# FNet block with modulated MLP on one core: the columns of 1+ca and sa turned by a 32x32 transpose, other buffers for the chunks of ga and sb, other assumed landing times

## The chip, the cores and the metric

The kernel runs on one core of a Trainium2 chip. A core has a matrix engine (TensorE, PE in the profile), a vector engine (VectorE, DVE), an activation engine (ScalarE, ACT), a general engine (GpSimd, POOL) and a synchronisation engine (SyncE, SP) that here only issues transfers (DMAs). Each engine takes its instructions in the order in which they were written. The metric is the device time of one execution in microseconds.

## The reference

```python
x = A_x                                              # 2048 x 1024
sa, ca, ga, sb, cb, gb = (silu(c) @ w_mod).reshape(6, 1024)
h = layernorm(x) * (1 + ca) + sa
x = x + ga * real(DFT_seq(DFT_hidden(h)))            # Cr@(h Dr) - Ci@(h Di)
h = layernorm(x) * (1 + cb) + sb
x = x + gb * (gelu(h @ w1 + b1) @ w2 + b2)           # 1024 -> 3584 -> 1024
```

Six rows of 1024 numbers, each a product of the vector silu(c) with 1024 columns of `w_mod`, scale and shift what the two large blocks work on. The DFT matrices (2048x2048 and 1024x1024, real and imaginary) are inputs.

## The kernel before, in words

**Stages on PE.** All matmuls are 128x128 by 128x512 in fp16, with operands split into a hi and a lo half. Stage 1 multiplies the normalised x by the DFT over the sequence, in four blocks of 512 output positions. Block 0 is done plainly (L1268): ops 0 to 15, 48 matmuls each. Blocks 1 to 3 are done in a scheme with seven products in place of eight (L1320): ops 16 to 99, 28 a block, 24 matmuls each. Then come the DFT over the hidden dimension (L1552) and the two matrix products of the MLP (L1735, L1844).

**What an op needs.** For every op a piece of the DFT matrix is loaded (`craw`, L801; `rawc`, L815), in blocks 1 to 3 combined on DVE (`comb_c`, L827; the sums are named T1 to T4), and split: ACT makes the hi half (L787), DVE the lo half (L790). PE starts an op when its lo half is there. Blocks 1 to 3 also read sums and differences of x: `s_tasks` makes them (DVE L753 to L756, ACT's hi half L764, DVE's lo half L767) and POOL stores them to DRAM (tiles `s_81` to `s_84`, L771), from where SP loads them again (L854). `u_tasks` does the like with the results of block 0 and later ones (ACT L897, DVE L900 and L912, POOL store L902).

**The modulation rows.** `pair_tasks(j, ...)` makes two rows of 1024 at a time: ca and sa (j = 0), ga and sb (1), A0 and A1 (2: the sa row carried through the hidden DFT), cb and gb (3). For each row SP loads eight raw chunks of 128x1024 (`load`, L499 from `w_mod`, L496 from the DFT), DVE multiplies each by a column of silu(c) and adds it up (`mul`: L503 the first, L505 the rest), and POOL adds the 128 partitions together in a tree of seven accumulating DMAs (L519: 64 rows on 64, 32 on 32, down to 1), then puts the rows to DRAM (`put`, L526). For j = 0, `get` (L539, L540) loads the two rows back as columns, one number of 4 bytes at a time, and one broadcast number (`m1`); `largest` (L545, L546), a reduction over partitions on POOL (L560) and `scales` (L549 to L556, with a helper at L203) scale them. Pair 2 needs the scaled columns.

The raw chunks go to places in one large SBUF tile, `arena`, by the table `RING`. A load waits until the previous user of its place is through (`used`, `free`, `was`). Chunks 6 and on of pair 1 (ga 6, ga 7, and of sb also the third and fourth of each four) use the places 184 and 188, where the rows of ca and sa stood; so they wait for the puts of ca and sa.

**What sets the order.** A planner on the host builds lists of `Task`s, each with an engine, a cost, what it depends on and a due time relative to PE (`t_op`). It picks tasks against a modelled clock and writes them out, engine by engine; what it assumes for the time from issue to landing of a transfer stands in `LANDS`. The order is fixed once the kernel is built; on the chip every instruction waits, with all behind it on its engine, until what it depends on is there.

Of the kernel before, what the change touches and what calls it, by code (L numbers as in the profile page):

```python
# [9 lines left out]
F32 = mybir.dt.float32  # L10
# [3 lines left out]
ALU = mybir.AluOpType  # L14
RED = bass_isa.ReduceOp
AX = mybir.AxisListType

P = 128
S = 2048
D = 1024  # L20
F = 3584
NS = S // P
ND = D // P
# [13 lines left out]
def kernel(ctx, tc, x, cre, cim, dre, dim, w1, b1, w2, b2, c, wm, out):  # L37
# [137 lines left out]
    def quad(g):  # L175
# [13 lines left out]
        [dram.tile([P, 4, 2, 512], F16, tag=f"dc_{m}_{ri}", name=f"dc_{m}_{ri}") for ri in range(2)] for m in range(7)  # L189
    ]  # L190
    arow_d = [dram.tile([1, D], F32, tag=f"arow_{n}", name=f"arow_{n}") for n in range(2)]
    row_d = {
        n: dram.tile([1, D], F32, tag=f"row_{n}", name=f"row_{n}") for n in ("ca", "sa", "ga", "sb", "cb", "gbb", "gb")
    }
    w1_d = [dram.tile([P, 7, 2, 512], F16, tag=f"w1_{g}", name=f"w1_{g}") for g in range(14)]
    w2_d = [dram.tile([P, 7, 2, 2, 512], F16, tag=f"w2_{v}", name=f"w2_{v}") for v in range(7)]
# [259 lines left out]


    scol, cc = mk([P, ND], F32, "scol"), mk([P, ND], F32, "cc")
    cols = mk([P, 2 * ND], F32, "cols")
    cs, csa = cols[:, 0:ND], cols[:, ND : 2 * ND]  # L460
    m1 = mk([P, 6], F32, "m1")
    ones = at(O_SO[0], 512)
# [1 line left out]
    def idle_pe(n):  # L464
# [8 lines left out]
    ROWS = (184, AUX[2], AUX[0], 64)  # L473
    RING = (
        [(192, 196, 172, 176, 180)[q % 5] if q < 10 else (192, 196)[q % 2] for q in range(16)],
        [(192, 196)[q % 2] if q < 6 else (192, 196, 184, 188)[q % 4] for q in range(16)],
        [(AUX[2], AUX[3], 64, 68)[q % 4] for q in range(16)],
        [AUX[q % 4] for q in range(16)],
    )
# [1 line left out]
    def pair_tasks(j, due, free):  # L481
# [6 lines left out]
        for q in range(2 * ND):  # L488
            i, k = divmod(q, ND)
            o = RING[j][q]  # L490
            name, b = names[i], at(o, 1024)
            col = csa if name in src else scol

            def load(name=name, k=k, b=b):
                if name in src:
                    sp.dma_start(b, dri[src[name]][:, k, :])  # L496
                else:
                    m = MODS.index(name)
                    sp.dma_start(b, wm[:, k, m * D : (m + 1) * D])  # L499

            def mul(i=i, k=k, b=b, col=col):
                if k == 0:
                    dve.tensor_scalar(rows[i], b, col[:, 0:1], None, op0=ALU.mult)  # L503
                else:
                    dve.scalar_tensor_tensor(rows[i], b, col[:, k : k + 1], rows[i], op0=ALU.mult, op1=ALU.add)  # L505

            loads.append(Task("dma", 1.5, load, [used.get(o) or free[o]], ("wm", name, k)))
            LANDS[loads[-1].key] = 4.0 if j else 6.0
            deps = [loads[-1].key, ("row", "sa", "end") if name in src else None]
            if k == 0:  # L510
                deps.append(free.get(place + 4 * i))
            muls.append(Task("dve", 1.3 if k else 0.75, mul, deps, ("row", name, k)))
            used[o] = muls[-1].key
# [4 lines left out]
        while n:  # L518
            f = lambda n=n: gp.dma_start(both[0:n], both[n : 2 * n], accum_op=ALU.add)  # L519
            t.append(Task("pool", 0.7, f, [last, muls[ND - 1].key], ("tree", j, n)))  # L520
            last = t[-1].key
            LANDS[last] = 3.0
            n //= 2

        def put(v, dst, dep, end=None):
# [2 lines left out]
            return u  # L528

        r = [v[0:1, :] for v in rows]  # L530
        row = [row_d[n][:, :] for n in names] if j != 2 else [a[:, :] for a in arow_d]
        if j == 0:
            t += [put(r[0], row[0], last, ("put", "ca")), put(r[1], row[1], last, ("put", "sa"))]
            dep = [t[-2].key, t[-1].key]

            def get():
                for name, o in (("ca", cs), ("sa", csa)):
                    v = row_d[name][0].rearrange("(k p) -> p k", p=P)
                    sp.dma_start(o, v, allow_slow_non_contiguous=True)  # L539
                sp.dma_start(m1[:, 4:5], row_d["ca"][0][0:1].partition_broadcast(P))  # L540

            m, pm, sd, iu = (m1[:, n : n + 1] for n in range(4))

            def largest():
                dve.tensor_scalar(cs, cs, 1.0, None, op0=ALU.add)  # L545
                dve.tensor_reduce(m, cols, axis=AX.X, op=ALU.max, apply_absolute_value=True)  # L546

            def scales():
                dve.tensor_scalar(m, m, 1e-30, None, op0=ALU.max)  # L549
                pow2(pm, m)  # L550
                dve.reciprocal(sd, pm)
                dve.tensor_scalar(sd, sd, SD, None, op0=ALU.mult)
                dve.tensor_scalar(iu, pm, 2.0**5 / SD, None, op0=ALU.mult)
                dve.tensor_scalar(cols, cols, sd, None, op0=ALU.mult)
                dve.tensor_scalar(m1[:, 4:5], m1[:, 4:5], 1.0, -1.0, op0=ALU.add, op1=ALU.mult)
                dve.tensor_scalar(m1[:, 4:5], m1[:, 4:5], sd, None, op0=ALU.mult)  # L556

            u = chain(
                ("dma", 1.5, get), ("dve", 0.4, largest),
                ("pool", 0.7, lambda: gp.partition_all_reduce(m, m, P, RED.absmax)), ("dve", 1.3, scales),  # L560
            )
            u[0].deps = tuple(dep)
            LANDS[u[0].key] = 6.0
            LANDS[u[2].key] = 1.0
            u[-1].key = ("row", "sa", "end")
            t += u
        elif j == 1:
            k_ = Task(
                "dve", 0.9, lambda: dve.tensor_scalar(r[0], r[0], m1[0:1, 3:4], None, op0=ALU.mult),
                [last, ("row", "sa", "end")],  # L570
            )
            t += [put(r[1], row[1], last), k_, put(r[0], row[0], k_.key, ("row", "sb", "end"))]
        elif j == 3:
            b = at(60, 1024)[0:1, :]
            l = Task("dma", 1.5, lambda: sp.dma_start(b, b2), [muls[-1].key])
            LANDS[l.key] = 5.0
            p = put(r[1], row[1], last)
            k_ = Task("dve", 0.9, lambda: dve.tensor_scalar(r[0], r[0], 1.0, None, op0=ALU.add), [last])
            m = Task("dve", 1.3, lambda: dve.tensor_tensor(b, b, r[1], op=ALU.mult), [l.key, last])
            t += [l, p, k_, put(r[0], row[0], k_.key), m, put(b, row_d["gbb"][:, :], m.key, ("row", "gb", "end"))]  # L580
        else:
            t += [put(v, o, last, ("row", n, "end")) for v, o, n in zip(r, row, names)]
# [346 lines left out]
    def d_tasks(n):  # L929
# [11 lines left out]
        for h in (1, 0):  # L941
            f = lambda h=h: sp.dma_start(b[h], dri[ri][:, c_ + 4 * h, :])
            ls.append(Task("dma", 1.5, f, [dep, ("row", "A0", "end") if n == 1 else ("g1", 15)]))
            LANDS[ls[-1].key] = 4.0
        if n % 4 == 0:
            dep = ("row", "A1", ND - 1) if n == 0 else ("dd", n - 1)
            z = Task("dma", 1.5, lambda: sp.dma_start(d0, dri[ri][0, 0].partition_broadcast(P)), [dep])
# [644 lines left out]
    load_halves([c0_raw(0)[:, 0:512], xf(8)], [cre[0, :, 0, :], x[8]])  # L1592
    sp.dma_start(c0_raw(0)[:, 512:1024], cre[0, :, 8, :])
    dve.memset(warm, 1.0)
    act.dma_start(cc[:, :], c)
    act.activation(warm[:, :], warm[:, :], AF.Silu)
    act.activation(scol[:, :], cc[:, :], AF.Silu)
# [38 lines left out]
                push("comb", "comb", cb_[kp][j], t_op(opn(tb, m, kp)) - (30.0, 25.0)[j])  # L1636
    pair_tasks(0, t_op(5), {o: ("op", 2) for o in RING[0]})
    was = {o: ("row", "sa", k) for o, k in ((192, 6), (196, 7))}
    was.update({184: ("put", "ca"), 188: ("put", "sa")})
    pair_tasks(1, t_op(9), {**was, AUX[2]: ("op", 6), AUX[3]: ("op", 7)})  # L1640
    s_end = {64: ("st", "s", 14), 68: ("st", "s", 15), AUX[0]: ("op", 14), AUX[1]: ("op", 15)}
    s_end.update({AUX[2]: ("row", "sb", "end"), AUX[3]: ("row", "sb", "end")})
# [379 lines left out]
    for kind, k in seq:  # L2022
# [47 lines left out]
        else:  # L2070
            v = k
# [59 lines left out]
```

## Time and profile before

| | us |
|---|---|
| median of 3 runs (lowest, highest) | 1990.1 (1988.07, 1990.2) |
| profiled execution, whole | 1989.65 |
| its span in the trace | 1987.7 |
| PE busy | 1939.7 (98%) |
| DVE busy | 1437.1 (72%) |
| ACT busy | 842.2 (42%) |
| POOL busy | 190.9 (10%) |
| stage 1, plain block: ops 2 to 15 | 33.29 to 196.90 |
| stage 1, blocks 1 to 3: ops 16 to 99 | 196.90 to 651.76 |

The granted clock of PE was 0.993 of full over the span. The page gives for each engine its busy time, for each wait the instruction that waited and the one that released it, and for DMAs the time from issue to landing. A timeline row has start, duration, engine, line, operation and, in brackets, the idle time ahead of it with its releaser. `SPq` is SP's queue of DMA issues: a long duration of three issues there means that one of them waited. Names like `arena<-in_wm_dram` read "written from".

### The profile page before, as it was taken

What the parts mean: (1) busy time and instruction counts of PE and PEld (TensorE: products, weight loads), DVE (VectorE), ACT (ScalarE), POOL (GpSimd) and SP (SyncE); (2) the same over time, 40 slices, a digit from 0 to 9 for tenths busy, and PEclk for the clock granted to TensorE, in tenths of its full rate; (3) what the DMA queues carried; (4) which work ended last, traced back from release to release, by engine and by line L of the source; (5) the groups of instructions that cost most, each with busy time, mean ns of one, the idle gap of its engine ahead of it and who ended that gap; (6) DMA issues with size and microseconds to landing.
All of it is one profiled execution on the core that took longest, in us unless ns stands there. A gap on an engine that the chain in (4) does not pass through costs nothing. (4 is left out here: it accounts for less than half of the span.)

```text
span 1987.7 us, 23757 instructions
## 1 busy us (share of the span) xinstructions
PE 1939.7 (98%) x8979; PEld 882.1 (44%) x8979; DVE 1437.1 (72%) x1872; ACT 842.2 (42%) x1081; POOL 190.9 (10%) x316
## 2 busy tenths in 40 slices
PE   9979989999999999999999999999999999999999
PEld 3434434444444444444444444444444444444444
DVE  8866787998885467877678998989873353553566
ACT  7522433544522345554577566456233312312311
POOL 0031212211101112211120000000000000000000
PEclk9999999999999999999999999999999999999999
DMA  8478798688787877868665555444477332432323
GB/s 331 156 241 265 244 334 282 242 288 291 257 310 259 322 244 269 297 222 300 261 229 178 179 196 175 138 170 151 168 229 213 118 97 83 127 101 69 112 75 85
DMA packets 146200, 412.92 MB, mean 208 GB/s; under 512 B 19115, under 2 KB 19179, under 8 KB 141998
## 3 DMA queue, kind: packets, MB, share of 16 engines
q1 hardware_dynamic: 117782, 316.23, 46.9%
q0 software_dynamic: 28160, 95.18, 14.3%
q8 instruction: 70, 1.15, 0.2%
q14 instruction: 44, 0.36, 0.1%
q10 hardware_dynamic: 144, 0.00, 0.0%
HBM read 271.88 MB, written 135.30 MB: 205 GB/s over the span
## 5 line engine op out<-in xcount | busy, mean ns | idle before, releaser
L1735 PE MATMUL ps<-arena 128*128 128x512 f16 x2352 | 511.9, 380 | 2.2 <-ACT arena L1757 2.2
L1844 PE MATMUL ps<-arena 128*128 128x512 f16 x2352 | 511.1, 379 | 2.7 <-DVE arena L1890 1.2
L1320 PE MATMUL ps<-arena 128*128 128x512 f16 x2016 | 439.5, 381 | 15.5 <-DVE arena L790 10.5
L1735 PEld LDWEIGHTS <-arena 128*128 128x128 f16 x2352 | 230.5, 98 | 280.7 <-issue 4.8
L1844 PEld LDWEIGHTS <-arena 128*128 128x128 f16 x2352 | 230.0, 98 | 281.3 <-issue 3.7
L1890 DVE SCALAR_TENSOR_TENSOR arena<-ps,i4c,arena 128x1024 f32<-128x1024 f32 x179 | 229.3, 1281 | 146.4 <-PE ps L1844 141.2
L1320 PEld LDWEIGHTS <-arena 128*128 128x128 f16 x2016 | 197.7, 98 | 257.2 <-issue 15.9
L1552 PE MATMUL ps<-arena 128*128 128x512 f16 x1344 | 294.0, 381 | 2.7 <-ACT arena L1568 2.7
L390 ACT ACTIVATE arena<-arena,shc 128x512 f16<-128x512 f32 (+1 forms) x115 | 116.0, 1018 | 282.2 <-PE ps L1844 189.2
L1552 PEld LDWEIGHTS <-arena 128*128 128x128 f16 x1344 | 131.9, 98 | 160.0 <-issue 5.3
L1268 PE MATMUL ps<-arena 128*128 128x512 f16 x768 | 169.2, 382 | 19.4 <-DVE arena L790 18.0
L415 DVE TENSOR_TENSOR arena<-arena 128x512 f32<-128x512 f32 (+1 forms) x228 | 171.1, 753 | 4.3
L402 DVE SCALAR_TENSOR_TENSOR arena<-arena,shc 128x512 f16<-128x512 f32 (+1 forms) x115 | 128.5, 1121 | 39.1 <-ACT arena L390 38.9
L787 ACT ACTIVATE arena<-arena 128x1024 f16<-128x1024 f32 x99 | 102.1, 1049 | 112.0 <-PE ps L1320 68.9
L1761 DVE TENSOR_TENSOR arena<-arena,ps 128x512 f32<-128x512 f32 x84 | 57.5, 684 | 110.9 <-PE ps L1735 107.1
L1754 ACT ACTIVATE arena<-arena,b1s,i1c 128x512 f32<-128x512 f32 x84 | 68.3, 813 | 138.3 <-DVE arena L1761 138.3
L1268 PEld LDWEIGHTS <-arena 128*128 128x128 f16 x768 | 75.1, 98 | 113.5 <-issue 21.9
L790 DVE SCALAR_TENSOR_TENSOR arena<-arena 128x1024 f16<-128x1024 f32 x99 | 118.8, 1217 | 8.0 <-ACT arena L787 7.8
L897 ACT ACTIVATE arena<-arena 128x1024 f16<-128x1024 f32 x56 | 58.6, 1052 | 113.5 <-DMA u<-arena 63.9
L900 DVE TENSOR_TENSOR arena<-arena 128x1024 f16<-128x1024 f32 x56 | 67.6, 1218 | 19.8 <-ACT arena L897 19.8
L390 ACT ACTIVATE arena<-arena,s1c 128x512 f16<-128x512 f32 (+1 forms) x70 | 60.9, 885 | 44.1 <-DVE arena L415 25.5
L402 DVE SCALAR_TENSOR_TENSOR arena<-arena,s1c 128x512 f16<-128x512 f32 (+1 forms) x70 | 66.4, 959 | 10.1 <-ACT arena L390 10.1
(165 smaller groups left out, 1384.9 us busy)
## 6 DMA issues: line engine op xcount, KB each, us to landing
w<-arena SPq DMA_DIRECT2D x64, 512.0 KB, 5.0
arena<-w SPq DMA_DIRECT2D x119, 256.0 KB, 2.7
u<-arena POOLq DMA_DIRECT2D x56, 512.0 KB, 5.9
arena<-u SPq DMA_DIRECT2D x112, 256.0 KB, 4.0
arena<-w SPq DMA_DIRECT2D x56, 512.0 KB, 3.4
arena<-in_wm_dram SPq DMA_DIRECT2D x48, 512.0 KB, 5.6
arena<-s SPq DMA_DIRECT2D x48, 512.0 KB, 6.1
arena<-in_cim_dram SPq DMA_DIRECT2D x32, 512.0 KB, 7.1
```

Source lines behind the costliest of these rows:

```text
L390: act.activation(o[m][0], q(j), AF.Copy, **sc)
L402: dve.scalar_tensor_tensor(o[m][1], q(j), scale, o[m][0], op0=ALU.mult, op1=ALU.subtract)
L415: dve.tensor_tensor(q(d), q(a), q(b), op=op)
L787: h = Task("act", 1.15, lambda: act.activation(o[:, :, 0], s2, AF.Copy, scale=SC), list(deps) + free)
L790: dve.scalar_tensor_tensor(o[:, :, 1], s2, SC, o[:, :, 0], op0=ALU.mult, op1=ALU.subtract)
L1268: pe.matmul(bank_of(d_), hleft(d_, s, kp, a), cop(n)[:, s, b], start=(kp == 0 and s == 0 and a == 0 and b == 0), stop=(kp == 7 and s == 1 ...
L1320: pe.matmul(bank_of(st + ch), left, cop(n)[:, s, b], start=(start and kp == 0 and s == 0 and a == 0 and b == 0), stop=(kp == 3 and s == 1 ...
L1552: pe.matmul(bank_of(bk), up(N)[:, c_, a], dp(n)[:, c_, w], start=(start and ri == 0 and c_ == 0 and i == 0), stop=(ri == 1 and c_ == 3 and ...
L1735: pe.matmul(ps.rearrange("p (k t) -> p k t", k=4), w1c[:, m, s, a, d * P : (d + 1) * P], zc(m)[:, b, :, d, :], start=(start and d == 0 and ...
L1754: act.activation(dst, src, AF.Gelu_apprx_tanh, scale=inv, bias=b1s[:, 2 * p + j : 2 * p + j + 1])
L1844: pe.matmul(t[:, j], hidc[:, c_, m, a, k * P : (k + 1) * P], w2c[:, m, c_, w], start=(start and c_ == 0 and n == 0), stop=(c_ == 1 and n = ...
L1890: lambda: dve.scalar_tensor_tensor(dst, ps[b], inv, dst, op0=ALU.mult, op1=ALU.add), kp[b],
```

## The change

It has three parts.

1. The rows ca and sa go to one DRAM tile `ca_d` of 2x1024. `get` loads them as eight DMAs of 8 rows by 128 bytes into a tile `turned` of 128x32, beside the broadcast as before. `largest` first transposes `turned` to `cols` on DVE, in blocks of 32x32, and the reduction and the scaling take the first 16 columns of it. `turned` is cleared once at the start.
2. The raw chunks of ga and sb go to the places 192, 196 and 216 in turn. 216 has no earlier user, and none of the loads waits for the puts of ca and sa.
3. `LANDS`, by which the planner orders, has for the chunks of the rows 7.0 us (before 4.0, for pair 0 6.0), for the levels of the tree 8.5 down to 2.5 (before 3.0 each), and 6.0 for the loads of the hidden DFT (before 4.0).

```diff
+    ca_d = dram.tile([2, D], F32, tag="ca_sa", name="ca_sa")
...
-    cols = mk([P, 2 * ND], F32, "cols")
+    turned, cols = mk([P, 32], F32, "turned"), mk([P, 32], F32, "cols")
...
-        [(192, 196)[q % 2] if q < 6 else (192, 196, 184, 188)[q % 4] for q in range(16)],
+        [(192, 196, 216)[q % 3] for q in range(16)],
...
-            LANDS[loads[-1].key] = 4.0 if j else 6.0
+            LANDS[loads[-1].key] = 7.0
...
-            LANDS[last] = 3.0
+            LANDS[last] = {64: 8.5, 32: 6.5, 16: 5.5, 8: 5.0, 4: 4.5, 2: 4.0, 1: 2.5}[n]
...
             def get():
-                for name, o in (("ca", cs), ("sa", csa)):
-                    v = row_d[name][0].rearrange("(k p) -> p k", p=P)
-                    sp.dma_start(o, v, allow_slow_non_contiguous=True)
-                sp.dma_start(m1[:, 4:5], row_d["ca"][0][0:1].partition_broadcast(P))
+                v = ca_d.rearrange("r (k q j) -> q r k j", q=4, j=32)
+                for q in range(4):
+                    for r_ in range(2):
+                        sp.dma_start(turned[32 * q + 8 * r_ : 32 * q + 8 * r_ + 8, :], v[q, r_])
+                sp.dma_start(m1[:, 4:5], ca_d[0][0:1].partition_broadcast(P))
...
             def largest():
+                dve.transpose(cols, turned)
                 dve.tensor_scalar(cs, cs, 1.0, None, op0=ALU.add)
-                dve.tensor_reduce(m, cols, axis=AX.X, op=ALU.max, apply_absolute_value=True)
+                dve.tensor_reduce(m, cols[:, 0 : 2 * ND], axis=AX.X, op=ALU.max, apply_absolute_value=True)
...
-            LANDS[ls[-1].key] = 4.0
+            LANDS[ls[-1].key] = 6.0
...
+    dve.memset(turned, 0.0)
...
-    was.update({184: ("put", "ca"), 188: ("put", "sa")})
+    was[216] = None
```

By the third part the planner's order changes on DVE, ACT, POOL and SP, from about op 4 of stage 1 to the end of stage 1; PE's does not. In the new kernel lines stand one to six further down: L505 is L506, L790 is L795, L767 is L772, L900 is L905, L912 is L917, L499 is L500, L815 is L820, L519 is L520, L771 is L776.

On DVE, around ops 12 and 13 (lo halves L790), ahead of the change. `scol` marks a multiplication of a raw chunk:

```order
L505 SCALAR_TENSOR_TENSOR arena_65<-arena_65,scol_190 128x1024
L790 SCALAR_TENSOR_TENSOR arena_65<-arena_65 128x2x512
L912 TENSOR_TENSOR arena_65<-arena_65 128x8x128
L755 TENSOR_TENSOR arena_65<-arena_65 128x512
L900 TENSOR_TENSOR arena_65<-arena_65 128x4x2x128
L545 TENSOR_SCALAR cols_192<-cols_192 128x8
L546 TENSOR_REDUCE m_6_193<-cols_192 128x1
L505 SCALAR_TENSOR_TENSOR arena_65<-arena_65,scol_190 128x1024
L503 TENSOR_SCALAR arena_65<-arena_65,scol_190 128x1024
```

And now, from op 12's half (the first L795) through op 13's (the second) to the columns:

```order
L795 SCALAR_TENSOR_TENSOR arena_65<-arena_65 128x2x512
L917 TENSOR_TENSOR arena_65<-arena_65 128x8x128
L506 SCALAR_TENSOR_TENSOR arena_65<-arena_65,scol_189 128x1024 x3
L905 TENSOR_TENSOR arena_65<-arena_65 128x4x2x128
L758 TENSOR_TENSOR arena_65<-arena_65 128x512
L917 TENSOR_TENSOR arena_65<-arena_65 128x8x128
L759 TENSOR_TENSOR arena_65<-arena_65 128x512
L795 SCALAR_TENSOR_TENSOR arena_65<-arena_65 128x2x512
L905 TENSOR_TENSOR arena_65<-arena_65 128x4x2x128
L506 SCALAR_TENSOR_TENSOR arena_65<-arena_65,scol_189 128x1024 x3
L549 STREAM_TRANSPOSE cols_192<-turned_191 128x32
L550 TENSOR_SCALAR cols_192<-cols_192 128x8
```

Before, `largest` stood between ops 12 and 13; now it stands, with the transpose, between ops 13 and 14, and six multiplications of raw chunks stand between op 12 and it.

On SP, from a pair of loads for time block 1 (`in_cre_dram 128x1024`; `in_wm_dram` marks the raw chunks) past the columns, before:

```order
L815 DMA arena_65<-in_cre_dram 128x1024 x2
L499 DMA arena_65<-in_wm_dram 128x1024 x3
L815 DMA arena_65<-in_cre_dram 128x1024 x2
L539 DMA cols_192<-row_ca 128x8x1
L539 DMA cols_192<-row_sa 128x8x1
L540 DMA m_6_193<-row_ca 128x1
L499 DMA arena_65<-in_wm_dram 128x1024 x2
L801 DMA arena_65<-in_cim_dram 128x2x512
L499 DMA arena_65<-in_wm_dram 128x1024 x5
```

and now:

```order
L500 DMA arena_65<-in_wm_dram 128x1024 x6
L820 DMA arena_65<-in_cre_dram 128x1024 x2
L806 DMA arena_65<-in_cim_dram 128x2x512
L500 DMA arena_65<-in_wm_dram 128x1024 x3
L543 DMA turned_191<-ca_sa 8x32 x8
L544 DMA m_7_193<-ca_sa 128x1
L806 DMA arena_65<-in_cim_dram 128x2x512
L500 DMA arena_65<-in_wm_dram 128x1024
```

Before, nine raw chunks of ga and sb were still to be loaded behind the columns; now one is.

On POOL, in tree 1 (the rows ga and sb), before:

```order
L519 DMA arena_65<-arena_65 64x2048
L519 DMA arena_65<-arena_65 32x2048
L519 DMA arena_65<-arena_65 16x2048
L771 DMA s_81<-arena_65 128x1024
L771 DMA s_82<-arena_65 128x1024
L771 DMA s_84<-arena_65 128x1024
L771 DMA s_83<-arena_65 128x1024
L519 DMA arena_65<-arena_65 8x2048
```

and now:

```order
L520 DMA arena_65<-arena_65 64x2048
L520 DMA arena_65<-arena_65 32x2048
L776 DMA s_81<-arena_65 128x1024
L776 DMA s_82<-arena_65 128x1024
L776 DMA s_84<-arena_65 128x1024
L776 DMA s_83<-arena_65 128x1024
L520 DMA arena_65<-arena_65 16x2048
L776 DMA s_81<-arena_65 128x1024
```

The four s stores went ahead of the tree's third level.

More of the change, by code (lines that the diff above doesn't have):

```diff
@@ L191 @@
     arow_d = [dram.tile([1, D], F32, tag=f"arow_{n}", name=f"arow_{n}") for n in range(2)]
+    ca_d = dram.tile([2, D], F32, tag="ca_sa", name="ca_sa")
     row_d = {
-        n: dram.tile([1, D], F32, tag=f"row_{n}", name=f"row_{n}") for n in ("ca", "sa", "ga", "sb", "cb", "gbb", "gb")
+        n: dram.tile([1, D], F32, tag=f"row_{n}", name=f"row_{n}") for n in ("ga", "sb", "cb", "gbb", "gb")
     }
@@ L530, in pair_tasks @@
         r = [v[0:1, :] for v in rows]
-        row = [row_d[n][:, :] for n in names] if j != 2 else [a[:, :] for a in arow_d]
+        row = [ca_d[i : i + 1, :] for i in range(2)] if j == 0 else (
+            [row_d[n][:, :] for n in names] if j != 2 else [a[:, :] for a in arow_d]
+        )
         if j == 0:
@@ L553, in scales @@
                 dve.tensor_scalar(iu, pm, 2.0**5 / SD, None, op0=ALU.mult)
-                dve.tensor_scalar(cols, cols, sd, None, op0=ALU.mult)
+                dve.tensor_scalar(cols[:, 0 : 2 * ND], cols[:, 0 : 2 * ND], sd, None, op0=ALU.mult)
                 dve.tensor_scalar(m1[:, 4:5], m1[:, 4:5], 1.0, -1.0, op0=ALU.add, op1=ALU.mult)
```

## The prediction

> **What bounds the kernel now.** I read the page's head first, then PE's waits, then PE's timeline, and only then the queues of the engines that PE waited for.
>
> ```profile
> span 1987.7 us, 23757 instructions
> PE 1939.7 (98%) x8979; PEld 882.1 (44%) x8979; DVE 1437.1 (72%) x1872; ACT 842.2 (42%) x1081; POOL 190.9 (10%) x316
> ```
>
> PE works for 98% of the span, so a change that removes no matmul can win only what PE idles, and what it runs slower after idling. The waits say where:
>
> ```profile
> PE ps L1268 <- DVE arena L790: 18.0, 4, 12.5
> PE ps L1320 <- DVE arena L790: 10.5, 5, 5.7
> PE ps L1320 <- DMA arena<-s: 4.9, 3, 2.1
> ```
>
> Columns: total us, times, longest. Nearly all of it is stage 1 waiting for an op's lo half (L790). The timeline puts the places:
>
> ```profile
> 33.29 104.08 PE L1268 MATMUL ps<-arena 128*128 128x512 f16 x480 [0.40 <-DVE arena L790]
> 149.91 12.37 PE L1268 MATMUL ps<-arena 128*128 128x512 f16 x48 [12.55 <-DVE arena L790]
> 165.92 31.13 PE L1268 MATMUL ps<-arena 128*128 128x512 f16 x143 [3.64 <-DVE arena L790]
> 196.90 36.93 PE L1320 MATMUL ps<-arena 128*128 128x512 f16 x169
> ...
> 257.30 18.45 PE L1320 MATMUL ps<-arena 128*128 128x512 f16 x72 [5.75 <-DVE arena L790]
> 282.27 10.30 PE L1320 MATMUL ps<-arena 128*128 128x512 f16 x47 [1.01 <-DVE arena L790]
> ...
> 389.74 262.18 PE L1320 MATMUL ps<-arena 128*128 128x512 f16 x1214
> 651.76 10.52 PE L1552 MATMUL ps<-arena 128*128 128x512 f16 x48
> ```
>
> Unhindered, ops 2 to 11 take 104.08/10 = 10.41 us for 48 matmuls, and the later run 262.18/1214 = 0.2160 us a matmul. Against that pace:
> - Loss A: from op 11's end (33.29 + 104.08 = 137.37) to 196.90 are 59.53 us for four ops, 41.6 at pace: 17.9 lost, 16.2 of it in the two waits and the rest in the slower 48 matmuls behind the longer one (12.37).
> - Loss B: from 196.90 to 651.76 are 454.86 us for 2016 matmuls, 435.4 at pace: 19.5 lost. Up to 282.27 (14 ops of 24, 72.6 at pace) it is 12.8; the other 6.7 come after.
>
> Together 37.4: more the change cannot win, since PE's own order and all work after 651.76 stay.
>
> Why op 12 is late stands in SP's queue, POOL's and DVE's:
>
> ```profile
> 117.94 24.13 SPq L499 DMA_DIRECT2D arena<-in_wm_dram  x3
> 143.13 0.51 SPq L539 DMA_DIRECT2D cols<-row_ca  x1
> 143.73 3.79 SPq L539 DMA_DIRECT2D cols<-row_sa  x1
> 147.56 4.81 SPq L540 DMA_DIRECT2D m<-row_ca  x1
> ```
>
> ```profile
> 140.01 0.52 POOL L526 DMA_DIRECT2D row_ca<-arena  x1 [1.98 <-DMA arena<-arena]
> ```
>
> ```profile
> 106.06 1.22 DVE L790 SCALAR_TENSOR_TENSOR arena<-arena 128x1024 f16<-128x1024 f32 x1
> 147.44 1.29 DVE L505 SCALAR_TENSOR_TENSOR arena<-arena,scol 128x1024 f32<-128x1024 f32 x1 [8.41 <-DMA arena<-in_wm_dram]
> 148.64 1.22 DVE L790 SCALAR_TENSOR_TENSOR arena<-arena 128x1024 f16<-128x1024 f32 x1
> 153.82 0.17 DVE L546 TENSOR_REDUCE m<-cols 128x1 f32<-128x16 f32 x1 [0.21 <-DMA cols<-row_sa]
> 157.82 1.28 DVE L505 SCALAR_TENSOR_TENSOR arena<-arena,scol 128x1024 f32<-128x1024 f32 x1 [3.83 <-DMA arena<-in_wm_dram]
> ```
>
> SP's third raw load here (chunk 6 of ga) sits until 142.1 (117.94 + 24.13) for the put of ca, whose row's place it takes. DVE's multiplication of that chunk starts at 147.44, and op 12's lo half stands right behind it. Then the element-wise column loads hold SP to 152.4; the next chunk is late by 3.83 more and op 13 (after a 3.64 wait at 165.92) with it.
>
> **The change, part by part.** *Other places.* Ga and sb chunks no longer wait for the puts of pair 0, so the waits of 8.41 and 3.83, and the 1.27 that follows, have no cause. What DVE then has to do before op 12 I take from the new order: nine instructions of 128x1024 (L767, L900, L912), four of 128x512, five L505 and one L503.
>
> ```profile
> L900 DVE TENSOR_TENSOR arena<-arena 128x1024 f16<-128x1024 f32 x56 | 67.6, 1218 | 19.8 <-ACT arena L897 19.8
> L755 DVE TENSOR_TENSOR arena<-arena 128x512 f32<-128x512 f32 x8 | 5.5, 690 | 0.2
> L505 DVE SCALAR_TENSOR_TENSOR arena<-arena,scol 128x1024 f32<-128x1024 f32 x42 | 53.9, 1282 | 24.0 <-DMA arena<-in_wm_dram 23.1
> L503 DVE TENSOR_SCALAR arena<-arena,scol 128x1024 f32<-128x1024 f32 x6 | 4.5, 748 | 1.3 <-DMA arena<-in_wm_dram 1.3
> ```
>
> 9 x 1.22 + 4 x 0.69 + 5 x 1.28 + 0.75 = 20.9 us, with op 12's own half 22.1. Op 11's half ended at 107.28; one L505 and one L767 more now stand ahead of it (2.5), so op 12 is ready at 107.28 + 2.5 + 22.1 = 131.9 if nothing waits; PE wants it at 137.37. The same count from op 12 to op 15 gives 10.1, 11.0 and 8.9 us, 30.0 in all against 31.2 on PE. So DVE has 5.5 us to spare, and waits are what remains:
>
> ```profile
> DVE arena L505 <- DMA arena<-in_wm_dram: 14.3, 3, 8.4
> DVE arena L767 <- ACT arena L764: 7.8, 2, 4.2
> ```
>
> From 109 to 166 us these and L503's 1.3 make 23.4; without the 13.5 named, 9.9 stay, and they lie ahead of op 12. If all stay, op 12 is 4.4 late and the slower clock behind a pause costs 12.37 - 10.41 = 2.0 on top, and some 2 at op 14: residual of A 0 to 8. I take 3, since the L767 waits are for s stores that POOL now issues earlier.
>
> *The transfers* must fit too.
>
> ```profile
> 95.00:180.00 85.00, 68.81 (x310) 30.53 (x308) 57.23 (x64) 23.64 (x25) 20.12 (x33) 0.92 0.79 261
> 180.00:233.00 53.00, 52.87 (x246) 23.86 (x244) 32.52 (x35) 22.37 (x27) 15.99 (x26) 1.00 0.66 186
> 233.00:303.00 70.00, 56.75 (x246) 24.47 (x245) 62.47 (x55) 20.77 (x21) 6.24 (x10) 0.95 0.97 344
> ```
>
> The last two columns are DMA share and GB/s. 85 x 0.79 = 67 us of full DMA work, now in 85 - 15 = 70 us: 0.96, no more than the 0.97 seen in the lowest row. It fits, barely, which is a second reason for 3 and not 0.
>
> *Columns.* Two element-wise loads become eight of 8x128 bytes and a transpose.
>
> ```profile
> cols<-row_ca SPq DMA_DIRECT2D x1, 4.0 KB, 10.2
> row_ca<-arena POOLq DMA_DIRECT2D x1, 4.0 KB, 1.6
> ```
>
> No such load is in the trace. Its landing lies between the contiguous 4 KB (1.6) and the element-wise one (10.2); I take 3, nearest the contiguous kind. SP's issue is 0.3 to 0.55 each (the 0.51 above), nine in 3 to 5 us instead of 9.2 (143.13 to 152.37). Tree 0 I leave ending as before, since between its levels there still stand groups of s and u stores: put at 140 to 142, columns at 148 to 150. `largest` and `scales` with what lies between need 5.5 us ahead of op 14's half, and PE wants op 14 at 137.37 + 2 x 10.41 = 158.2: they must be there by 151.5. Two us to spare; cost 0, up to 7 with the longer landing. The transpose (128x32) lies between the reduction's 0.17 and the 0.69 of 128x512; I take 0.2, hidden in DVE's spare time, and 0.7 at most without it. The new memset runs beside the first loads, 0.1 if uncovered.
>
> The Trainium skill speaks against this part ("DMA: Bandwidth & Descriptors", section "Rules for kernel authors"): many small transfers are to be made one, since little ones pay mostly overhead. The same table says that a strided last dimension lowers to one descriptor per element, which is for the change; the 10.2 above agrees. The page's section "Anatomy of one DMA" gives about 2 us fixed for each DMA from GpSimd; for nine in series an estimate from it is 18 us.
>
> *Assumed landings.* They alter the order of DVE, ACT, POOL and SP up to some 640 us. What of it reaches PE I see in POOL's queue before stage T3 of time block 1:
>
> ```profile
> 188.76 0.80 POOL L519 DMA_DIRECT2D arena<-arena  x1 [7.59 <-DMA arena<-arena]
> 194.25 0.78 POOL L519 DMA_DIRECT2D arena<-arena  x1 [4.69 <-DMA arena<-arena]
> 195.24 2.24 POOL L771 DMA_DIRECT2D s<-arena  x4 [0.21 <-issue]
> ```
>
> ```profile
> 200.66 1.23 DVE L767 TENSOR_TENSOR arena<-arena 128x1024 f16<-128x1024 f32 x1 [8.77 <-ACT arena L764]
> ```
>
> Four s stores stand behind tree 1's third level; ACT cannot reuse their buffer, and DVE waits 8.77 for ACT. In the new order they stand behind the second level: not at 195.24 but between the start of that level's issue (188.76) and its end (189.56), so 5.7 to 6.5 sooner; I take 6, and as much of the wait goes. So DVE reaches its unbroken stretch (62.47 of 70 us busy from 233 to 303) about 6 us earlier against PE. Its work up to op 29 counts the same in both orders to half a us. The 12.8 then shrink to 6.8. The later 6.7 hang on loads of s and of the hidden-DFT matrix that wait for PE or come when DMA is full; I leave them. Residual of B: 13.5. Its ends: 19.5 (nothing won) and 4 (little but the 4.9 of waits for s).
>
> *Sum*, from the profiled execution (1989.65 us, its span and 1.95 around it, 0.45 below the median 1990.1): 17.9 - 3 + 19.5 - 13.5 = 20.9, so 1968.75; with the 0.45, 1969.
>
> **Rivals.**
> 1. *A is won, B is not.* PE comes to time block 1 some 15 us sooner, while transfers there already run at 0.97 and DVE at 62.47 of 70. Then 1990.1 - 15 = 1975, or 1980 if A keeps 8 and B gives 0. For it: nothing is removed from DVE's or DMA's work there. Against: DMA had only 0.66 from 180 to 233. The Trainium skill's same page, section "Bandwidth", has HBM per core bind at about 358 GB/s; by that the 24.1 MB of the 70 us (70 x 344 GB/s) take at least 67 us, an estimate that would leave 3 of the 12.8 to win in place of 6. The 344 agrees with such a limit.
> 2. *B is nearly emptied.* DVE's lead lasts through time block 1: residuals 2 and 4, 1990.1 - 31.4 = 1958. Against: the rows 257.30 and 282.27 show PE waiting for a DVE that the windows show busy nine tenths.
> 3. *Eight small loads in series.* If each of nine pays an issue of 0.5 and a landing of 1.6 one behind the other, 2.1 each, columns are there at 143 + 19 = 162 and op 14's half at 167.5, 9 late; with 2 for the clock behind the pause 20.9 - 11 = 9.9 are left, 1980. Against: the three loads of before did not wait for each other's landing (issues 143.13 and 143.73, landings of 10). It decides once columns land after 151.5. The coalescing rule cited above is this rival.
> The next rival rests on two rows of SP:
>
> ```profile
> SPq L496 <- DMA row_ga<-arena: 8.3, 1, 8.3
> ```
>
> ```profile
> 227.18 0.80 SPq L496 DMA_DIRECT2D arena<-in_dre_dram  x2
> ```
>
> 4. *Slower: tree 1 comes late.* Groups of s stores now stand between its levels. If four of them hold POOL as long as the 8.77 above, 35 us, row ga, which ought to come 17 us earlier than before, comes 18 later; A0's and A1's multiplications on DVE stand ahead of ops 26 to 29, and PE has them to wait for. With 8 us of cover (SP waited as long for row ga unpunished) the loss is 10 beyond the whole gain: 2000. It decides once row ga is later than before by the clock of the span, where SP's loads that wait for it came at 227.
> 5. *Nothing changes*: DMA swallows all of A; 1989.
>
> **How the numbers follow.** Likeliest as summed 0.55 (own range 1960 to 1977: residual A 0 to 8 with B 7 to 18); rival 1 0.20, rival 2 0.12, rival 3 0.07, rival 4 0.04, rival 5 0.02. From 1957 to 1982 lie the likeliest case, rivals 1 and 3 and most of 2; some 0.15 stays outside. A measurement of this kernel tells 0.2%, 4 us. Faster 0.91; same 0.05 (rival 5 and the slow edges of 1 and 3); slower 0.04.
>
> **What would show it.** Right: no wait over 4 us in PE's row for L1268; SP's loads of ga and sb without a wait for the put of ca; op 16 starting at 179 to 187; the eight small loads over in 5 us and the transpose at 148 to 152, near 0.2 us; the first matmul of L1552 near 630. Wrong: DVE waiting for raw chunks ahead of op 12 though their places are free (A's residual), PE's waits for L790 after op 16 still 10 us or more (rival 1), the reduction after 152 (rival 3), or row ga landing later than 227 (rival 4).

## The result, and the profile after

The changed kernel takes 1967.4 us (median of 4 runs, 1965.9 to 1968.5) against 1989.1 for the one before (median of 4): a ratio of 0.9894, with an interval of 0.9876 to 0.9911. The prediction said 1969, and its range held the time. The profiled execution took 1967.3 us with a span of 1965.5, to be held against 1989.65 and 1987.7.

PE's waits after, in us in total, times, longest:

```profile
PE ps L1325 <- DVE arena L795: 8.3, 7, 5.2
PE ps L1273 <- DVE arena L795: 6.7, 3, 4.8
...
PE ps L1325 <- DMA arena<-s: 0.8, 1, 0.8
```

L1273 is the line that was L1268 and L1325 the one that was L1320; the 18.0 of the plain block are now 6.7, and the sum of the three rows has gone from 33.4 to 15.8. PE's timeline says where the rest is:

```profile
85.50 71.83 PE L1273 MATMUL ps<-arena 128*128 128x512 f16 x332 [0.31 <-DVE arena L643]
162.13 22.35 PE L1273 MATMUL ps<-arena 128*128 128x512 f16 x95 [4.79 <-DVE arena L795]
184.31 52.18 PE L1325 MATMUL ps<-arena 128*128 128x512 f16 x241
...
288.19 132.02 PE L1325 MATMUL ps<-arena 128*128 128x512 f16 x602 [5.19 <-DVE arena L795]
...
631.79 10.52 PE L1557 MATMUL ps<-arena 128*128 128x512 f16 x48
```

Ops 12 and 13 run through in one piece with what is ahead of them (the row from 85.50); the pause of 12.55 us is gone. Of the pauses over 1 us one is left at op 14 and one at op 34. The hidden DFT starts at 631.79, 20.0 us sooner; 1.7 of the other 2.2 us of the span (8 us at a clock lower by 0.21) are a drop of the clock that came behind a pause of 2.67 us before and stayed out behind one of 2.46 now; the last section has the rows.

Why op 14 still waits stands in three queues. SP, POOL and DVE after:

```profile
116.50 15.12 SPq L500 DMA_DIRECT2D arena<-in_wm_dram  x6
...
151.24 3.45 SPq L543 DMA_DIRECT2D turned<-ca_sa  x8
154.73 0.35 SPq L544 DMA_DIRECT2D m<-ca_sa  x1
```

```profile
125.41 0.86 POOL L520 DMA_DIRECT2D arena<-arena  x1 [8.94 <-DMA arena<-arena]
...
149.63 1.01 POOL L527 DMA_DIRECT2D ca_sa<-arena  x2 [3.98 <-DMA arena<-arena]
```

```profile
134.59 1.22 DVE L795 SCALAR_TENSOR_TENSOR arena<-arena 128x1024 f16<-128x1024 f32 x1
...
156.05 0.21 DVE L549 STREAM_TRANSPOSE cols<-turned 128x32 f32<-128x32 f32 x1 [5.52 <-DMA turned<-ca_sa]
...
160.85 1.22 DVE L795 SCALAR_TENSOR_TENSOR arena<-arena 128x1024 f16<-128x1024 f32 x1
```

The loads of ga and sb run on without the 24 us hold, and op 12's half is ready at 135.8, in time. But tree 0's rows are put at 149.63, not at 140.01 as before: from the fourth level's issue to the put it takes 24.2 us in place of 14.9 (from 125.07). The columns come at 156.05, and op 14's half (the second L795 row) stands behind them. DMA is fuller while the tree runs; the last two columns of these rows, before and after, are DMA share and GB/s:

```profile
125.00:140.00 15.00, 12.36 (x58) 5.49 (x56) 9.71 (x9) 4.79 (x5) 6.08 (x9) 1.00 0.41 128
```

```profile
125.00:150.00 25.00, 25.00 (x117) 11.37 (x116) 24.00 (x22) 5.79 (x6) 7.06 (x11) 1.00 0.90 324
```

It is tempting to put that down to the raw chunks, which now move at the same time, but a run of the next section speaks against them as the only cause. With the landings alone, SP issues no raw chunk between 116.3 and 154.38, and the row of ca is put just as late:

```profile
114.67 1.65 SPq L499 DMA_DIRECT2D arena<-in_wm_dram  x2
...
154.38 2.42 SPq L499 DMA_DIRECT2D arena<-in_wm_dram  x4
```

```profile
149.65 0.52 POOL L526 DMA_DIRECT2D row_ca<-arena  x1 [6.50 <-DMA arena<-arena]
```

There the same stretch (127.57 to 149.65) takes 22.1 us at a DMA share of 0.81, from other loads and from POOL's stores, whose places between the levels had changed as well. How much of the delay comes from the chunks, from the other traffic and from the order on POOL, the runs don't separate.

### The profile page after: what moved, and what is told of

Same layout as the page of the kernel before. It is cut to its first block, busy times and chain, and to the rows that moved or that the text cites. A ratio compares the mean times of both kernels' runs of the same rounds, so it can differ in the third digit from the quotient of the medians.

```text
span 1965.5 us, 23771 instructions
## 1 busy us (share of the span) xinstructions
PE 1935.7 (98%) x8979; PEld 881.5 (45%) x8979; DVE 1437.9 (73%) x1874; ACT 841.8 (43%) x1081; POOL 191.2 (10%) x316
## 4 chain that ended last, share of the span: by engine, by line
PE 43%; DVE 4%; issue 1%; DMA 1%; ACT 1%; SPq 0%; DVEq 0%; ACTq 0%
PE ps L1850 22%; PE ps L1741 21%; DVE arena L403 1%; DVE arena L1896 1%; DVE arena L416 1%; DMA arena<-in_w_dram 1%; ACT arena L391 0%; DVE arena L1940 0%; DMA w<-arena 0%; DVE arena L1767 0%; DVE arena L401 0%; ACT ps L1053 0%; ACT arena L1760 0%; DVE arena L1890 0%; ACT arena L1886 0%
## 5 line engine op out<-in xcount | busy, mean ns | idle before, releaser
L1325 PE MATMUL ps<-arena 128*128 128x512 f16 x2016 | 438.5, 380 | 9.1 <-DVE arena L795 8.3
L1325 PEld LDWEIGHTS <-arena 128*128 128x128 f16 x2016 | 197.6, 98 | 249.9 <-issue 12.8
L1273 PE MATMUL ps<-arena 128*128 128x512 f16 x768 | 168.8, 382 | 8.0 <-DVE arena L795 6.7
L795 DVE SCALAR_TENSOR_TENSOR arena<-arena 128x1024 f16<-128x1024 f32 x99 | 119.1, 1219 | 15.5 <-ACT arena L792 15.4
L1273 PEld LDWEIGHTS <-arena 128*128 128x128 f16 x768 | 75.2, 98 | 101.6 <-issue 9.8
L905 DVE TENSOR_TENSOR arena<-arena 128x1024 f16<-128x1024 f32 x56 | 67.8, 1220 | 23.3 <-ACT arena L902 23.2
```

The source lines that it names most:

```text
L795: dve.scalar_tensor_tensor(o[:, :, 1], s2, SC, o[:, :, 0], op0=ALU.mult, op1=ALU.subtract)
L1273: pe.matmul(bank_of(d_), hleft(d_, s, kp, a), cop(n)[:, s, b], start=(kp == 0 and s == 0 and a == 0 and b == 0), stop=(kp == 7 and s == 1 ...
L1325: pe.matmul(bank_of(st + ch), left, cop(n)[:, s, b], start=(start and kp == 0 and s == 0 and a == 0 and b == 0), stop=(kp == 3 and s == 1 ...
```

## The experiments

The theory at the start was the prediction's: the other places remove the waits at ops 12 to 15 (loss A), the assumed landings help time block 1 (loss B), the columns cost nothing. The first rival: the assumed landings do it all, through the order. The tables give the us that PE loses against the pace of the prediction, in the profiled execution of each kernel: from op 2 to op 16 (less 14 x 10.41), from op 16 to op 30 (less 72.6) and from op 30 to the hidden DFT's first matmul (less 1680 x 0.2160), each from first matmul to first matmul. By this count the kernel before loses 18.6, 11.4 and 8.0; the prediction began loss A at op 11's end and cut loss B at op 30's second matmul, hence its 17.9, 12.8 and 6.7. One execution of columns alone, whose order is that of before, differs from before by up to 2.9 in a column, so smaller differences say little.

### Each part alone

Places alone: the kernel before with

```diff
-        [(192, 196)[q % 2] if q < 6 else (192, 196, 184, 188)[q % 4] for q in range(16)],
+        [(192, 196, 216)[q % 3] for q in range(16)],
-    was.update({184: ("put", "ca"), 188: ("put", "sa")})
+    was[216] = None
```

> The kernel before with part 2 alone (ga's and sb's chunks in places 192, 196 and 216). Theory (the places cure the waits for raw chunks, the assumed landings cure time block 1): the wait of 12.5 us at op 12 goes; but with the old landings the planner puts the columns' reduction right behind op 12's half, so op 13 waits for columns that land at 152 to 160: 6 to 12 us of loss A stay, loss B (19.5) stays: 1980 to 1984. Rival (the landings did it all, the places alone only move the wait): 1987 to 1990.

Landings alone: the kernel before with

```diff
-            LANDS[loads[-1].key] = 4.0 if j else 6.0
+            LANDS[loads[-1].key] = 7.0
-            LANDS[last] = 3.0
+            LANDS[last] = {64: 8.5, 32: 6.5, 16: 5.5, 8: 5.0, 4: 4.5, 2: 4.0, 1: 2.5}[n]
-            LANDS[ls[-1].key] = 4.0
+            LANDS[ls[-1].key] = 6.0
```

> The kernel before with part 3 alone (assumed landings). Its order puts the chunk that waits for the put of ca, and the columns, behind op 15. Theory: loss A shrinks to about 3 by the order alone, but the chunks still come late, so tree 1 and row ga end later than 227 and A0's multiplications hold ops 26 and on: B grows by 5 to 10: 1980 to 1985. Rival (true landings are the whole gain, the places nothing): 1966 to 1970.

Columns alone: the kernel before with the new `ca_d`, `turned`, `get` and the transpose.

> The kernel before with part 1 alone; all engines keep the order of before but for the column loads and the transpose. Theory: SP is held 4 us and not 9.2, columns land some 7 us sooner after the put; the 12.5 at op 12 stays, the 3.6 at op 13 goes with part of the slower clock: 1984 to 1987. Rival (small loads one behind the other, or the column path hidden): 1989 or 1990.

And the changed kernel with the old `get` and no transpose, so places and landings:

> The changed kernel with the element-wise column loads of before; all engines keep the order of the changed kernel. Theory: the columns stand ahead of op 14's half, and it waits for them already with the small loads (4.8 us on PE); 10 us of landing in place of about 2, and 9 us of SP in place of 4, make op 14 some 7 us later: 1973 to 1976. Rival (the column path costs nothing, since the row's put is what is late): 1967 to 1968.

| kernel | median us | ratio to before (interval) | lost to op 16 | to op 30 | to the hidden DFT |
|---|---|---|---|---|---|
| places alone | 1994.6 | 1.0028 (1.0013 to 1.0042) | 22.1 | 13.7 | 10.9 |
| landings alone | 1963.6 | 0.9878 (0.9856 to 0.9901) | 5.2 | 4.2 | 6.5 |
| columns alone | 1987.4 | 1.0004 (0.9994 to 1.0014) | 18.2 | 13.8 | 5.1 |
| places and landings | 1965.3 | 0.9888 (0.9873 to 0.9903) | 7.5 | 1.5 | 7.9 |
| all three | 1967.4 | 0.9894 (0.9876 to 0.9911) | 7.0 | 2.7 | 9.3 |

The first rival is right: the landings alone give the whole gain, in both losses, and a little more than the rival's own numbers (1966 to 1970). The places alone make the kernel slower, beyond what either theory said, and the columns do nothing that can be measured, alone or in the changed kernel. Places alone, PE and DVE:

```profile
143.94 13.47 PE L1268 MATMUL ps<-arena 128*128 128x512 f16 x48 [6.64 <-DVE arena L790]
166.92 32.75 PE L1268 MATMUL ps<-arena 128*128 128x512 f16 x143 [9.50 <-DVE arena L790]
```

```profile
152.36 0.17 DVE L545 TENSOR_SCALAR cols<-cols 128x8 f32<-128x8 f32 x1 [8.47 <-DMA cols<-row_ca]
```

The 12.55 at op 12 has become 6.64 there and 9.50 at op 13: the planner, still believing that a level of the tree lands in 3 us, now put the columns right behind op 12's half, and DVE waits there with all that stands behind. The waits of the prediction are replaced rather than removed: the 8.41 for a chunk ahead of op 12 is gone, the 8.47 for the columns stands in the row above, and a wait of 3.46 for a chunk is left ahead of op 13 (at 159.38). Ahead of op 12 DVE waits 4.21 and 1.38 us for ACT (at 133.48 and 136.08), and three multiplications of chunks stand there. With the landings alone, the chunk of ga still waits for the put, but its multiplication and the columns stand behind op 15's half, where nobody is held by them:

```profile
85.54 92.33 PE L1268 MATMUL ps<-arena 128*128 128x512 f16 x427 [0.15 <-DVE arena L638]
182.76 75.43 PE L1320 MATMUL ps<-arena 128*128 128x512 f16 x336 [4.89 <-ACT arena L1244]
```

Ops 7 to 15 run in one piece. The 4.89 that is left is another thing: ACT's copies of block 0's results (L1244) use the same memory as some places of the chunks and rows, and had to wait for DVE's multiplications:

```profile
182.12 1.08 ACT L1244 ACTIVATE arena<-ps 128x512 f32<-128x512 f32 x2 [9.81 <-DVE arena L505]
```

The columns: the hold of SP that the prediction blamed on element-wise loads is there with the eight small ones too, and it is absent with element-wise ones in another place of the queue. Columns alone, and then places and landings with the old loads:

```profile
142.85 9.13 SPq L543 DMA_DIRECT2D turned<-ca_sa  x8
```

```profile
151.54 0.39 SPq L539 DMA_DIRECT2D cols<-row_ca  x1
152.04 0.66 SPq L539 DMA_DIRECT2D cols<-row_sa  x1
```

```profile
cols<-row_ca SPq DMA_DIRECT2D x1, 4.0 KB, 3.1
```

9.13 us for the eight, 9.6 with the broadcast, where two element-wise loads and the broadcast took 9.2; 0.4 and 0.7 us, and 3.1 to land, where the prediction had read 10.2 as their price. So what held SP at 143 us went with the place in the queue and not with the kind of load. Which transfers ahead did it, the runs don't show.

The Trainium skill's rule on many small transfers ("DMA: Bandwidth & Descriptors", "Rules for kernel authors") did not decide here either: from the first of the eight issues (151.24) to the transpose that needs them all (156.05) are 4.8 us. The 18 us of the prediction's estimate rest on a figure that the same page of the Trainium skill ("Anatomy of one DMA") gives for DMAs from GpSimd, and these are issued by SP.

### Which landings

Tree's levels alone, and raw chunks alone, each in the kernel before:

```diff
-            LANDS[last] = 3.0
+            LANDS[last] = {64: 8.5, 32: 6.5, 16: 5.5, 8: 5.0, 4: 4.5, 2: 4.0, 1: 2.5}[n]
```

> The kernel before with the assumed landings of the tree's levels alone (8.5 down to 2.5 in place of 3 each). In its order chunk 6 of ga and the columns' reduction stand behind op 15's half on DVE, as with all the landings. Theory (loss A goes since nothing that hangs on tree 0 stands ahead of ops 12 to 15): no wait over 2 us in PE's row for L1268, A's 17.9 down to 4 or 5, B 10 to 16: 1966 to 1974. Rival (the loads' landings are what matters): 1985 to 1990.

```diff
-            LANDS[loads[-1].key] = 4.0 if j else 6.0
+            LANDS[loads[-1].key] = 7.0
```

> The kernel before with the assumed landings of the raw chunks alone (7 us). Its order keeps the columns' reduction right behind op 12's half, ahead of op 13. Theory: op 13 waits for columns as before, A keeps 10 to 18, B moves by 5 at most: 1982 to 1990. Rival (loads believed later are enough): 1966 to 1972.

| kernel | median us | ratio to before (interval) | lost to op 16 | to op 30 | to the hidden DFT |
|---|---|---|---|---|---|
| tree's levels alone | 1976.7 | 0.9941 (0.9917 to 0.9964) | 7.7 | 13.2 | 11.6 |
| raw chunks alone | 1969.5 | 0.9908 (0.9886 to 0.9931) | 9.7 | 6.9 | 3.8 |

Tree's levels alone cut loss A to 7.7 where 4 or 5 were expected, with a pause of 4.53 at op 12 where none over 2 was; B rose from 19.4 to 24.8 where 10 to 16 were expected. The time is 3 us above the range. The raw chunks alone, expected to do little, gave three quarters of what all landings give, and the rival's time (1966 to 1972):

```profile
155.09 32.47 PE L1268 MATMUL ps<-arena 128*128 128x512 f16 x143 [7.50 <-DVE arena L790]
```

```profile
145.68 0.17 DVE L545 TENSOR_SCALAR cols<-cols 128x8 f32<-128x8 f32 x1 [6.93 <-DMA cols<-row_ca]
```

The columns do stand ahead of op 13 and hold it, as said; but op 12 no longer waits, since chunk 6 of ga went behind it, and tree 0 ended sooner (put at 138.3), so that the columns came at 145.7 and not at 153.4. The expectation had only counted the order at op 13. In the total the two add up to about what all landings give (8.6 and 15.9 us apart, 24.3 together, by the medians), but not stage by stage (A: 10.9 and 8.9 apart, 13.4 together). The third figure, 6.0 for the loads of the hidden DFT, was not tried by itself.

### What is left at op 14

The changed kernel, with the columns held back to behind op 15:

```diff
             u[0].deps = tuple(dep)
+            u[1].deps = (u[0].key, ("op", 15))
```

> The changed kernel, the columns' transpose and reduction made to depend on op 15, so that they stand behind its half on DVE. Theory (what is left of loss A, 6.2 us, is op 14's half standing behind columns that land at 156): the 4.8 wait at op 14 goes with its slower clock, op 16 starts at 179 to 180: 1961 to 1963. Rival (PE loses it elsewhere, to evictions that wait for sb's last chunk or to row ga): 1966 to 1969.

It took 1953.0 us, 0.9827 of before (0.9803 to 0.9850). The losses are 2.8, 3.8 and 3.7: PE waits nowhere for more than 1.9 us in stage 1, and its clock never drops (granted clock 1.0). Tree 0 is put just as late there (150.38), and the pause at op 14 is gone, so the mechanism at op 14 is shown. What it is worth by itself is not, since the one dependency also moved other work of DVE and ACT. The gain over the changed kernel is 14 us by the medians and not the expected 4 to 6. The profiled execution, the slowest of its four (1957.6), gains 9.7, of which the table has 4.2 up to op 16 and 5.6 in the last column (9.3 to 3.7), less 1.1 between them; why the later loss shrank, and the rest, was not followed.

```profile
170.06 10.30 PE L1274 MATMUL ps<-arena 128*128 128x512 f16 x47 [1.60 <-DVE arena L796]
180.20 36.64 PE L1326 MATMUL ps<-arena 128*128 128x512 f16 x169
```

Can the planner do that by itself, if it is told what the changed kernel's trace has for tree 0?

```diff
-            LANDS[last] = {64: 8.5, 32: 6.5, 16: 5.5, 8: 5.0, 4: 4.5, 2: 4.0, 1: 2.5}[n]
+            LANDS[last] = {64: 10.0, 32: 10.5, 16: 10.0, 8: 5.5, 4: 7.5, 2: 6.5, 1: 5.0}[n]
```

> The changed kernel with the tree's landings as its own trace has them for tree 0 (10, 10.5, 10, 5.5, 7.5, 6.5, 5 us in place of 8.5, 6.5, 5.5, 5, 4.5, 4, 2.5). The planner itself then puts the columns behind op 15. Theory (a planner that is told later landings keeps late things out of PE's way): as with the columns moved by hand at op 14, 1961 to 1964, if time block 1 does not lose by it. Rival (landings that are too long for tree 1 put off row ga and the multiplications with it): 1967 to 1975.

1973.4 us, 0.9928 (0.9910 to 0.9946): 6 us slower than the changed kernel, though stage 1 loses only 0.2, 0.4 and 6.2. It is the rival's number, but not by the rival's cause, since only 0.4 is lost from op 16 to op 30. The loss is in the hidden DFT:

```profile
PE ps L1459 <- ACT arena L1442: 17.9, 1, 17.9
...
883.57 1.97 PE L1459 MATMUL ps<-ident,arena 128*128 128x128 f32 x8 [17.88 <-ACT arena L1442]
```

The order of ACT and DVE had changed there too, 700 us further on. The next kernel gives the longer landings to trees 0 and 1 alone, which leaves the order from the hidden DFT on word for word that of before:

```diff
+            LANDS[last] = ({64: 10.0, 32: 10.5, 16: 10.0, 8: 5.5, 4: 7.5, 2: 6.5, 1: 5.0} if j < 2
+                else {64: 8.5, 32: 6.5, 16: 5.5, 8: 5.0, 4: 4.5, 2: 4.0, 1: 2.5})[n]
```

> Like tree_real, but only trees 0 and 1 get the longer landings; trees 2 and 3 keep those of the change, and the order from the hidden DFT on is word for word that of before. Theory (tree_real won stage 1 and lost 18 us only because the planner, told of late trees 2 and 3, mixed other work into the hidden stage): stage 1 as in tree_real (lost at ops 12 to 15 under 1 us, in all under 8), no wait of 18 us at L1459: 1950 to 1955. Rival (PE, arriving 12 us earlier, outruns transfers and DVE in the hidden stage): the stall stays in part, 1963 to 1973.

1956.8 us, 0.9843 (0.9828 to 0.9858), 2 us above the upper end expected. The 17.9 is gone, and PE runs from op 10 far into time block 2 without a pause:

```profile
109.63 68.37 PE L1273 MATMUL ps<-arena 128*128 128x512 f16 x316
177.84 212.79 PE L1325 MATMUL ps<-arena 128*128 128x512 f16 x985
```

So it was the reshuffled order and not PE's earlier arrival that cost 18 us. The same idea once more, for the broadcast load for which DVE waited ahead of op 34 in the changed kernel (the expectation says 33):

```diff
-            LANDS[z.key] = 4.0
+            LANDS[z.key] = 11.0
```

> real2 with 11 us in place of 4 for the broadcast load of the hidden DFT's first row (d0), for which DVE waited 6.7 us ahead of op 33 in the changed kernel. Theory: DVE takes it later, PE loses 1 to 3 us less in time block 1: 1948 to 1953. Rival (it isn't on PE's path once DVE has a lead): as real2 within 2 us.

1968.5 us, 0.9903 (0.9886 to 0.9919): 12 us slower than without it. Up to op 30 nothing is lost, as without it (0.2 and -0.1); then 12.7 in place of 8.9, and 6.4 at the start of the hidden DFT:

```profile
PE ps L1325 <- DVE arena L795: 8.8, 5, 4.8
PE ps L1557 <- ACT arena L1573: 6.4, 1, 6.4
```

Both theories fall. The planner's order changed with the one figure, and PE waits in other places; which work came in its way was not followed.

### The order by hand, and the places with the columns out of the way

Two last tests of how far the order at ops 12 to 15 goes. First the kernel before with nothing but two added dependencies:

```diff
+            if j == 1 and q >= 6:
+                deps.append(("op", 15))
...
+            u[1].deps = (u[0].key, ("op", 15))
```

> The kernel before, places and landings as they were; by two added dependencies the multiplications of ga's chunks 6 and on and the columns' reduction stand behind op 15's half. Theory (loss A is a matter of DVE's order alone): no wait over 3 us at L1268, A lost 4 to 6; B keeps its 19.5 or a little more, since ga's row comes later: 1972 to 1980. Rival (the chunks still wait, and the wait only moves behind op 15): 1986 to 1992.

1993.6 us, 1.0028 (1.0018 to 1.0038). Loss A falls to 10.2, but B rises from 19.4 to 38.3 (13.9 and 24.4). The total is 2 us above the rival's range, and comes about by a way that the rival did not name. PE's waits for the lo halves of time blocks 1 to 3 are now eleven:

```profile
PE ps L1323 <- DVE arena L793: 19.6, 11, 4.2
```

```profile
225.60 0.48 POOL L528 DMA_DIRECT2D row_ga<-arena  x1 [0.18 <-issue]
```

Row ga is put at 225.60, 5.9 us later than before (219.68), while PE is 8.9 us further (op 16 at 187.96). With the landings alone it is put later still, at 231.68, and little is lost in B. What the two have apart is the rest of the order. Which rows of it make the 24.4 was not followed further, and stays open.

Then parts 1 and 2 with the old landings, the columns behind op 15 by the same dependency:

> Parts 1 and 2 of the change with the old landings, and the columns behind op 15 by an added dependency. Theory (the places cure the chunk waits, and ring_only was slow because the columns stood ahead of op 13): op 13's wait of 9.5 goes, op 12's of 6.6 stays in part, B as in ring_only: 1976 to 1984. Rival (the chunks, loaded earlier, are what puts work in front of op 12): 1988 to 1995.

1995.0 us, 1.0039 (1.0024 to 1.0054), as with the places alone: the rival's number. DVE, and SP's wait:

```profile
159.08 3.93 DVE L506 SCALAR_TENSOR_TENSOR arena<-arena,scol 128x1024 f32<-128x1024 f32 x3 [12.81 <-DMA arena<-in_wm_dram]
```

```profile
SPq L543 <- DMA ca_sa<-arena: 16.2, 1, 16.2
```

With the old landings the issue of the column loads stands ahead of three raw chunks in SP's queue, waits 16.2 us for the put, and the chunks wait with it; their multiplications stand ahead of op 13. The place of a chunk is free, but the queue isn't. In the changed kernel a single chunk is left behind the column loads, and that was the landings' doing.

## Why the prediction was right, and where it wasn't

**The time was right, 1969 against 1967.4; the attribution was not.** The step that failed is the one headed *Other places*: "ga and sb chunks no longer wait for the puts of pair 0, so the waits of 8.41 and 3.83, and the 1.27 that follows, have no cause". The places by themselves cost some 6 us (0.28%): DVE's wait moved to the columns, ahead of op 13. The landings alone give 0.988 without them, the same within the intervals. The number came out because its count (131.9 for op 12's half, measured 135.8; PE wanted it at 136.5) was made on the new order, which the landings had made. It was the order that took out the late work; the places were given the credit.

That the time came within 2 us is in part luck. Stage 1 from op 2 on won 19.1 us and not 20.9: A kept 3.2 more than was taken for it, B 1.4 less. Another 0.9 came ahead of op 2 and 2.2 behind stage 1, where the prediction had put nothing.

**Loss A, residual 3.** By the prediction's count it is 6.2 (from op 11's end at 136.5 to 184.31, less 41.6), inside its 0 to 8. The term that was mis-sized is tree 0, "I leave ending as before": the put came 9.6 us later. So the columns passed the limit of 151.5 that the third rival had named, but not by its cause: the eight loads were issued in 3.45 us and the transpose took 0.21, as estimated (3 to 5, and 0.2). Two of the signs that the prediction named for being right failed by this: PE's longest wait in the plain block was 4.8 and not under 4, and the transpose came at 156.05 and not at 148 to 152.

**Columns.** Bounded by the row of 10.2 us and SP's 9.2, both misread: they belong to the place in the queue. The cost of 0 was right. SP is held shorter in the changed kernel (3.8 us for the nine), but the old three loads take 2.7 at the same place, so the small loads aren't the reason. Nor is 10.2 the price of an element-wise load, since one landed in 3.1 there, and it is no support for the rule that the prediction saw it agree with.

**Transfers.** "It fits, barely" was right: from 95 to 180 the DMA share was 0.84 and op 12 did not wait for a chunk. What was missed is that tree 0 would take longer in the new order, at the fuller DMA.

**Loss B, residual 13.5.** Measured 447.5 - 435.4 = 12.1 (184.31 to 631.79). The direction was right and the size too small: the first of the sums T3 starts 21.2 us behind op 16 and no longer 32.2 (rows 205.55 and 229.13 of DVE's timeline), 11 sooner and not 6, and the loss up to op 30 is 2.7 and not 6.8. The mechanism is only in part the one foretold. Between op 16 and T3 DVE is idle for 6.5 us and no longer 13.4, and has 14.7 us of work ahead of it and no longer 18.9. Its waits for ACT there, from which the prediction took the 6 us, fell from 7.9 to 6.3 alone. More came from a row that it didn't name: a wait for tree 1 stood ahead of T3, and now that row stands behind the first sums, with no wait. Before and after:

```profile
215.23 0.74 DVE L569 TENSOR_SCALAR arena<-arena,m 1x1024 f32<-1x1024 f32 x1 [5.24 <-DMA arena<-arena]
```

```profile
213.12 0.73 DVE L574 TENSOR_SCALAR arena<-arena,m 1x1024 f32<-1x1024 f32 x1
```

On the other side the later part, left at 6.7, is 9.4: DVE waits 6.7 us for the broadcast load ahead of op 34, and PE 5.19 for that.

**Rivals.** None of the five was right as it stood. The 344 GB/s of the first is no ceiling for this mix of traffic: rows of the last section have 400 and 419. The fourth's point of decision, row ga later than 227, was passed in the run with the landings alone (put at 231.68), and that kernel is among the fast ones: a late row did little harm in that order.

## What to carry to other kernels

Where a planner writes a fixed order for queues that run in order, its assumed durations are part of the kernel: telling it that something lands late moves what depends on it out of the way, which the freed buffers here did not. Test the parts of such a change apart, since a new order makes every part look useful. And look at the order far behind the edit: some microseconds more in a table, for trees 2 and 3, moved work in the hidden DFT and cost 18, and a later landing for one load cost 12.

The best versions found are the changed kernel with the columns behind op 15 (0.9827) and the one with longer landings for the first two trees (0.9843); their intervals overlap with each other, and neither with the changed kernel's.

## What the runs showed of the hardware that was not expected

A queue's hold says little of what is held: eight loads of 1 KB took SP 9.13 us at one place and 3.45 at another, an element-wise one 0.66 and, in the kernel before, 3.79.

A short pause can cost clock, and need not. Before, PE's pause of 2.67 us at the start of the hidden DFT was followed by a stretch at a lower granted clock (0.79 in the row below, third column from the right); after, one of 2.46 at the same place was not:

```profile
664.00:672.00 8.00, 7.04 (x25) 2.87 (x25) 4.99 (x5) 3.02 (x4) 1.38 (x3) 0.79 1.02 419
```

```profile
640.00:660.00 20.00, 17.54 (x82) 7.88 (x81) 11.98 (x11) 7.91 (x9) 2.67 (x5) 1.00 1.01 400
```

The Trainium skill ("TensorE: Matmul & The Clock Gate", "What's actually happening") has the clock halve after an idle window of about 3.4 us, and the window free-running; here shorter pauses were enough: the 2.67, and pauses of 2.2 near the start of the MLP's first matrix product, before and after (they end at 1002.39 and 980.53), each with a mean clock of 0.79 over the 8 us from 1003 and from 981. The 3.64 at op 13 before was followed by a clock of 1.00 (165.92 to 176). How idle a window has to be, no run here shows.
